# A fused attention + MLP block on one core: new order of the head, of the hidden-layer units and of the second half, and layer normalisation moved from VectorE to GpSimd

## The chip, the cores and the metric

The kernel runs on one core of a Trainium2 chip, in one launch. The metric is the device time of the launch in microseconds (us). Before the change, three runs gave a median of 188.48 us (188.34 to 201.64). One further run was taken with the hardware profiler; all trace times in this document are counted from the start of its span.

## The reference, cut to what matters

One input x of 2048 tokens by 512 channels, in bfloat16, is normalised, then goes through a linear attention with 32 heads of 16 channels and through a two-layer MLP with 1792 hidden units. Both results are added to x.

```python
xn = layernorm(x)                                # no scale, no bias
q, k, v = split(xn @ wqkv)                       # 32 heads x 16
pq, pk  = q @ w_phi[h], k @ w_phi[h]             # 16 x 16 per head
phi     = concat(softmax(+p), softmax(-p))       # for pq and for pk
kv, z   = phi_k.T @ v, sum over tokens of phi_k  # per head
attn    = (phi_q @ kv) / (phi_q . z + 1e-6)
out     = x + attn @ wo + mish(xn @ w1 + b1) @ w2
```

## The kernel before, in words

The 2048 tokens are 16 tiles of 128 (one tile in the 128 partitions), in four groups of four. The program is an order written out by hand: each engine executes its instructions strictly in the order in which the code issues them, and only semaphores between engines, and the reuse of buffers, make an engine wait. So the place of a call in the code is its place in every queue.

**The parts.** `ln_stats` (L110) takes mean and variance of some tiles on VectorE (two `bn` instructions a tile) and the reciprocal root on GpSimd (an add, L119, and a power, L122). `ln_apply` (L125, L127) writes the normalised tile `xn`, one VectorE instruction a tile. `xn` is turned into `xnT` either by TensorE (`ln_turn_pe`, four transposes and a copy; group 0) or by a DMA transpose of two tiles on SP's queue (`ln_turn_dma`, L145; groups 1 to 3). `load_turned` (L87) loads a 512 x 512 part of `wqkv` transposed by DMA (`wT`), and `fold` (L93) multiplies it with the block-diagonal `w_phi` (`Wbd`), so that one projection gives the softmax logits: `wkp` for keys, `wqp` for queries.

**Slots.** The softmaxes run in eight slots `s` of four tiles: slots 0 to 3 are the keys of groups 0 to 3, slots 4 to 7 the queries. `logits(s, i)` is one tile's projection (four matmuls of 512 columns) and a copy out of PSUM; `extremes(s)` (L194) finds maxima and minima of 16 and subtracts them (ten VectorE instructions); `exponentials(s)` (L223) is two ScalarE instructions of 128 x 2048, and for query slots also issues DMA transposes of the results (`qT`, L235) on SP; `normalise(s, k)` (L240) divides by the sums on VectorE; `accumulate(g)` (L274) adds a group's keys and values into PSUM (`pkv`). `value(t)` projects v. `hidden(n)` (L168) takes the next n of 56 *units* of the first MLP layer: four matmuls of 512 columns and one ScalarE Mish each. ScalarE reloads its table at each change between Exp and Mish.

**The second half.** `mask_kv` takes the sums out of PSUM. For each pair of tiles `h`: `attend(h, i)` (L312) multiplies `qT` with the sums (eight short matmuls into the one buffer `pnd`) and ScalarE copies the result out in four instructions (L332 to L339); `combine(h)` (L341) divides numerator by denominator in seven VectorE instructions and issues a DMA transpose of the result (`ob`, L373); `second_layer(t)` (L375) is 14 matmuls of 512 columns into a PSUM bank `po`; `project_out(h)` (L384) adds the output projection into the two banks and `residual` (L394) adds x on VectorE and issues the output's DMA.

**Buffers that matter.** One pool of five PSUM banks (tag `mm`) is shared by `fold`, transposes, `project`, `hidden` and `second_layer`: TensorE waits when the bank five allocations back hasn't been copied out. `pkv` and `pnd` share one buffer.

**Order around the change.** In the head, SP's queue issues x tiles 0-1, the transposed `wT`, x tiles 4-7, `wv`, `w1`, x tiles 8-15; ScalarE's queue issues `w_phi`, x tiles 2-3 and `b1`. TensorE runs 12 matmuls on an identity (L437), then `fold`, the turning of tiles 0 and 1, `logits(0, 0)`, tiles 2 and 3, `logits(0, 1..3)`, `value(0..3)`, `hidden(4)`. The main loop is L481, with `hidden((16, 14, 8, 10, 4)[s])`; each slot's VectorE work holds the layer normalisation of the group two ahead (of group 1 in `extremes(0)`, L472). The second half starts at L509.

Of the kernel before, what the change touches and what calls it, by code (L numbers as in the profile page):

```python
# [17 lines left out]
def kernel(  # L18
# [68 lines left out]
    def load_turned(base_col):  # L87

        wT = lnp.tile([P, 4, 512], BF16, name="wT", tag="xn")
        nc.sync.dma_start_transpose(out=wT[:], in_=A_wqkv[:, base_col : base_col + D])  # L90
        return wT

    def fold(wT, dst, dve):  # L93

        for kt in range(KT):
            pf = ps.tile([P, 512], FP32, name="pfold", tag="mm")
            for j in range(4):
                nc.tensor.matmul(
                    pf[:, j * P : (j + 1) * P],
                    lhsT=wT[:, j, kt * P : (kt + 1) * P],  # L100
                    rhs=Wbd[:, j, :],
                    start=True,
                    stop=True,
                )
# [236 lines left out]
    def combine(h):  # L341

        nm, ds = nd_of.pop(h)
        ds = ds[:].rearrange("p i l x j h -> p i l x (j h)")
        u = opool.tile([P, 2, 2, 32], FP32, name="u")
        w = opool.tile([P, 2, 32], FP32, name="w")
        f = opool.tile([P, 2, 2, 32, 2], BF16, name="f")
        ob = lnp.tile([P, 4, 512], BF16, name="ob", tag="xn")
        o_t = ob[:, 0:2, :]
        oT_of[h] = ob[:, 2:4, :].rearrange("p i (j c) -> p (i j) c", c=P)  # L350
        nc.vector.tensor_tensor(  # L351
            out=u[:], in0=ds[:, :, :, 0, :], in1=ds[:, :, ::-1, 1, :], op=ALU.mult
        )
        nc.vector.tensor_tensor(out=w[:], in0=u[:, :, 0, :], in1=u[:, :, 1, :], op=ALU.add)
        nc.vector.reciprocal(w[:], w[:])  # L355
        nc.vector.tensor_tensor(
            out=u[:], in0=ds[:, :, ::-1, 1, :],
            in1=w[:, :, None, :].to_broadcast([P, 2, 2, 32]), op=ALU.mult,
        )
        nc.vector.tensor_copy(  # L360
            f[:].rearrange("p i l c o -> p (i l c) o"),
            u[:].rearrange("p i l (c o) -> p (i l c) o", o=1).to_broadcast([P, 128, 2]),
        )
        v = nm.rearrange("p i l (c e o) -> p (i l c) e o", e=8, o=2)
        nc.vector.tensor_tensor(  # L365
            out=v, in0=v,
            in1=f[:].rearrange("p i l c o -> p (i l c) o")[:, :, None, :].to_broadcast([P, 128, 8, 2]),
            op=ALU.mult,
        )
        nc.vector.tensor_tensor(  # L370
            out=o_t, in0=nm[:, :, 0, :], in1=nm[:, :, 1, :], op=ALU.add
        )
        nc.sync.dma_start_transpose(out=oT_of[h], in_=o_t.rearrange("p i c -> p (i c)"))  # L373

    def second_layer(t):  # L375
        po = ps.tile([P, 512], FP32, name="po", tag="mm")
        po_of[t] = po
        for f in range(FT):
# [4 lines left out]

    def project_out(h):  # L384
        for i in range(2):
            po = po_of.pop(2 * h + i)
            for j in range(4):
                nc.tensor.matmul(  # L388
                    po[:], lhsT=oT_of[h][:, i * 4 + j, :], rhs=wo_sb[:, j, :],
                    start=False, stop=(j == 3),  # L390
                )
            residual(2 * h + i, po)

    def residual(t, po):  # L394
        y = x_sb[:, t, :]
        nc.vector.tensor_tensor(out=y, in0=po[:], in1=y, op=ALU.add)  # L396
        nc.sync.dma_start(o_v[:, t, :], y)


    nc.sync.dma_start(x_sb[:, 0:2, :], x_v[:, 0:2, :])  # L400
    with nc.allow_non_contiguous_dma(reason="tiny w_phi load"):
        nc.scalar.dma_start(wsrc[:], wphi_v)
# [33 lines left out]
    for _ in range(12):  # L436
        nc.tensor.matmul(  # L437
            warm[:], lhsT=ident[:], rhs=ident[:, None, :].to_broadcast([P, 4, P]),
            start=True, stop=True,
        )  # L440
# [138 lines left out]
```

## Time and profile before

| | |
|---|---|
| median of three runs | 188.48 us |
| the profiled execution's own time | 188.35 us |
| its span (first to last instruction) | 186.6 us |
| TensorE busy | 176.2 us, 94% of the span |
| VectorE busy | 148.4 us, 80% |
| ScalarE busy | 127.0 us, 68% |
| GpSimd busy | 8.2 us, 4% |
| data moved by DMA | 18.02 MB |
| table loads of ScalarE | 13 of 1.283 us |

Busy TensorE time counts from the start of a matmul to its modelled end, and matmuls overlap, so a busy engine is not yet one at its peak. A dense stream of matmuls of 512 columns starts one every 0.216 us in this trace (32 in 6.91 us). What can be gained is therefore in the gaps, and these are read from the waits of TensorE, from the chain of work that ended last, and from the timeline around each gap.

### The profile page before, as it was taken

To read this page: it belongs to the slowest core of one execution; us is meant where nothing else is said; L and a number is where in the kernel's file an instruction comes from. 1 tells how busy PE (TensorE), PEld (TensorE's weight loads), DVE (VectorE), ACT (ScalarE), POOL (GpSimd) and SP (SyncE) were. 2 spreads that over 40 slices of the span, in tenths; PEclk is the share of its full clock that TensorE was granted. 3 is DMA by queue.
4 is the path that set the end of the run, shared out by engine and by line. 5 is a ranking of instruction groups with operands and counts; after the bars stand their busy time and mean duration, and the time that the engine had idled before them with its cause. 6 is when DMAs were issued, how large, how long until landed. Compare 5 with 4: busy or idle time off the path is not lost.

```text
span 186.6 us, 2710 instructions
## 1 busy us (share of the span) xinstructions
PE 176.2 (94%) x1021; PEld 88.5 (47%) x1021; DVE 148.4 (80%) x255; ACT 127.0 (68%) x196; POOL 8.2 (4%) x22
## 2 busy tenths in 40 slices
PE   6699879999999999999999999799999999999982
PEld 2444334464444654644464555355554545455430
DVE  4989999978999899989997927299947696738742
ACT  2458999889887899969969859573842567244200
POOL 3403020000200000000000000000000000000000
PEclk9999999999999999999999999999999999999998
DMA  6996999000190000000002900973079303980732
GB/s 146 304 404 222 209 358 164 0 4 2 34 191 0 4 0 0 0 0 4 0 0 53 176 0 0 179 160 60 0 170 192 87 5 66 196 189 1 116 84 84
DMA packets 44217, 18.02 MB, mean 97 GB/s; under 512 B 36780, under 2 KB 43692, under 8 KB 44204
## 3 DMA queue, kind: packets, MB, share of 16 engines
q1 hardware_dynamic: 43376, 17.57, 40.1%
q10 hardware_dynamic: 828, 0.28, 0.6%
q8 instruction: 8, 0.13, 0.3%
q14 instruction: 5, 0.04, 0.1%
HBM read 6.84 MB, written 2.10 MB: 48 GB/s over the span
## 4 chain that ended last, share of the span: by engine, by line
PE 76%; DVE 9%; ACT 6%; DMA 5%; issue 1%; ACTq 0%; SPq 0%
PE ph L174 24%; PE pproj L154 20%; PE po L379 18%; PE po L388 6%; PE pkv L279 4%; PE pnd L323 4%; DMA ob<-ob 3%; ACT e L226 2%; DMA x_sb<-in_A_x_dram 2%; DVE stats L116 1%; DVE wv L365 1%; ACT acts L181 1%; DVE ob L370 1%; DVE w L355 1%; ACT wv L332 1%
## 5 line engine op out<-in xcount | busy, mean ns | idle before, releaser
L379 PE MATMUL po<-w_sb,acts 128*128 128x512 bf16 x224 | 50.8, 379 | 0.0
L174 PE MATMUL ph<-xnT,w_sb 128*128 128x512 bf16 x224 | 49.5, 379 | 1.2 <-ACT p_sb L192 1.2
L181 ACT ACTIVATE acts<-ph,b1f 128x512 bf16<-128x512 f32 x56 | 35.5, 694 | 3.8 <-PE ph L174 3.5
L174 PEld LDWEIGHTS <-w_sb 128*128 128x128 bf16 x224 | 21.9, 98 | 27.5 <-issue 1.4
L226 ACT ACTIVATE e<-e 128x2048 bf16<-128x2048 bf16 x16 | 29.7, 1902 | 7.0 <-DVE e L216 6.9
L379 PEld LDWEIGHTS <-acts 128*128 128x128 bf16 x224 | 21.4, 98 | 23.1
L154 PEld LDWEIGHTS <-xnT 128*128 128x128 bf16 x192 | 18.4, 98 | 22.9 <-DMA xnT<-xn 1.3
L192 ACT CAST p_sb<-pproj 128x512 bf16<-128x512 f32 x29 | 15.7, 586 | 9.7 <-PE pproj L154 9.7
L244 DVE TENSOR_REDUCE s<-e 128x128 f32<-128x2048 bf16 x8 | 18.2, 2279 | 1.6 <-ACT e L226 1.6
L396 DVE TENSOR_TENSOR x_sb<-po,x_sb 128x512 bf16<-128x512 f32 x16 | 10.6, 685 | 7.6 <-PE po L388 7.6
L388 PE MATMUL po<-wqk,ob 128*128 128x512 bf16 x64 | 15.1, 379 | 0.7 <-DMA ob<-ob 0.7
L154 PE MATMUL pproj<-wkp,xnT 128*128 128x512 bf16 x64 | 14.7, 379 | 0.8 <-DMA xnT<-xn 0.8
L154 PE MATMUL pproj<-wv,xnT 128*128 128x512 bf16 x64 | 15.1, 379 | 0.0
L332 ACT CAST wkp<-pnd 128x768 bf16<-128x768 f32 x8 | 6.4, 798 | 12.6 <-PE pnd L323 8.7
L154 PE MATMUL pproj<-wqk,xnT 128*128 128x512 bf16 x64 | 14.6, 379 | 0.2 <-DVE x_sb L396 0.2
L205 DVE TENSOR_TENSOR m<-p_sb 128x1024 bf16<-128x1024 bf16 x16 | 11.0, 686 | 3.9 <-ACT p_sb L192 3.9
L351 DVE TENSOR_TENSOR u<-ds 128x128 f32<-128x128 f32 x8 | 2.3, 289 | 12.8 <-ACT ds L339 12.8
L205 DVE TENSOR_TENSOR m<-m 128x512 bf16<-128x512 bf16 (+1 forms) x32 | 11.5, 358 | 1.1
L323 PE MATMUL pnd<-kvm,qT 128*128 128x144 bf16 x128 | 10.6, 226 | 1.1 <-ACT ds L339 1.1
L323 PEld LDWEIGHTS <-qT 128*128 128x128 bf16 x128 | 9.1, 98 | 5.0 <-issue 1.3
L116 DVE BATCH_NORM_STATS2 stats<-x_sb 128x6 f32<-128x512 bf16 x16 | 10.0, 680 | 1.2 <-DMA x_sb<-in_A_x_dram 1.2
L332 ACT CAST wv<-pnd 128x768 bf16<-128x768 f32 x8 | 6.3, 792 | 6.1 <-PE pnd L323 3.8
(64 smaller groups left out, 173.0 us busy)
## 6 DMA issues: line engine op xcount, KB each, us to landing
w_sb<-in_B_w_dram SPq DMA_DIRECT2D x2, 1792.0 KB, 8.7
out_dram<-x_sb SPq DMA_DIRECT2D x16, 128.0 KB, 1.9
x_sb<-in_A_x_dram SPq DMA_DIRECT2D x1, 1024.0 KB, 11.4
x_sb<-in_A_x_dram SPq DMA_DIRECT2D x1, 512.0 KB, 4.1
wv<-in_A_wqkv_dram SPq DMA_DIRECT2D x1, 512.0 KB, 5.0
wqk<-in_A_wo_dram SPq DMA_DIRECT2D x1, 512.0 KB
x_sb<-in_A_x_dram SPq DMA_DIRECT2D x1, 256.0 KB, 3.1
x_sb<-in_A_x_dram ACTq DMA_DIRECT2D x1, 256.0 KB, 3.5
```

Source lines behind the costliest of these rows:

```text
L116: nc.vector.bn_stats(stats[:, i, :], x_sb[:, t0 + i, :])
L154: nc.tensor.matmul(pp[:], lhsT=xnT[:, t, kt, :], rhs=w[:, kt, :], start=(kt == 0), stop=(kt == KT - 1),)
L174: nc.tensor.matmul(ph[:], lhsT=w1_sb[:, kt, f * P : (f + 1) * P], rhs=xnT[:, g * TPG : (g + 1) * TPG, kt, :], start=(kt == 0), stop=(kt == ...
L181: nc.scalar.activation(acts[:, f, g * 512 : (g + 1) * 512], ph[:], ACT.Mish, bias=b1f[:, f : f + 1])
L192: copy(p_of[s][:, i, :], pp[:])
L205: nc.vector.tensor_tensor(out=m[:], in0=src[:, :, 0:half], in1=src[:, :, half : 2 * half], op=op)
L226: nc.scalar.activation(v, v, ACT.Exp)
L244: nc.vector.reduce_sum(t[:], v.rearrange("p t l (c e) -> p (t l c) e", e=16), axis=AX.X)
L323: nc.tensor.matmul(blocks(pnd, pl, j, 144), lhsT=qT_of[h][:, i, pl * 4 + j, :], rhs=kvm[:, pl, j, :], start=True, stop=True,)
L332: nc.scalar.copy(to[:, :, 0:3, :], a)
L379: nc.tensor.matmul(po[:], lhsT=acts[:, f, t * P : (t + 1) * P], rhs=w2_sb[:, f, :], start=(f == 0), stop=False,)
L388: nc.tensor.matmul(po[:], lhsT=oT_of[h][:, i * 4 + j, :], rhs=wo_sb[:, j, :], start=False, stop=(j == 3),)
```

## The change

- **Head.** `wT` is loaded in two halves, one on SP's and one on ScalarE's DMA queue. In the built program SP's half carries a wait for the completion of ScalarE's half, and all that SP issues later stands behind it: x tiles 2-3, `wv`, x tiles 4-7, `b1`, `w1`, x tiles 8-15 (`b1` and x tiles 2-3 were on ScalarE's queue). The identity matmuls become 8. Three small copies go from VectorE to GpSimd. The four tiles of group 0 are normalised in three steps (tile 0, tile 1, tiles 2-3), with a ScalarE square root and a VectorE reciprocal instead of GpSimd's power. Tile 0 is turned between the second and third step of `fold`; `logits(0, 0)`, `logits(0, 1)` and `value(0)` come before tiles 2 and 3 are turned. `fold`'s fourth copy stays on VectorE, ahead of tile 1's normalisation.
- **Units.** `hidden` takes 5, then 19, 14, 8, 8, then 2 (before: 4, then 16, 14, 8, 10, then 4). Two of the four copies of `logits(1)` go to VectorE.
- **Normalisation.** `ln_apply` of groups 1 to 3 runs on GpSimd.
- **Second half.** `attend(0, 0)` and `attend(0, 1)` stand before `extremes(5)`, with `second_layer(1)` cut in two around the latter. `combine(3)` stands behind `project_out(2)` and no longer before it. `combine(7)` is cut into two tiles, the first before `project_out(5)`. The last tile's output projection, residual and output are cut into two halves of 256 columns, and the first half's output goes out on ScalarE's queue.

```diff
-    def load_turned(base_col):
+    def load_turned(base_col, queues=(nc.sync,)):
         wT = lnp.tile([P, 4, 512], BF16, name="wT", tag="xn")
-        nc.sync.dma_start_transpose(out=wT[:], in_=A_wqkv[:, base_col : base_col + D])
+        n = D // len(queues)
+        for i, queue in enumerate(queues):
+            queue.dma_start_transpose(
+                out=wT[:, :, i * n : (i + 1) * n],
+                in_=A_wqkv[i * n : (i + 1) * n, base_col : base_col + D],
+            )
...
-    def fold(wT, dst, dve):
+    def fold(wT, dst, dve, behind={}):
...
+            if kt in behind:
+                behind[kt]()
...
-    def ln_apply(t0, n, mv, rstd, xn, at):
+    def ln_apply(t0, n, mv, rstd, xn, at, engine=nc.vector):
         for i in range(n):
-            nc.vector.tensor_scalar(
+            engine.tensor_scalar(
...
-    def combine(h):
+    def combine(h, parts=(slice(0, 2),)):
...
+        for q in parts:
...
+            nc.sync.dma_start_transpose(
+                out=oT_of[h][:, 4 * q.start : 4 * q.stop, :],
+                in_=o_t[:, q].rearrange("p i c -> p (i c)"),
+            )
...
     def project_out(h):
         for i in range(2):
             po = po_of.pop(2 * h + i)
...
+            cuts = (slice(0, 256), slice(256, 512)) if (h, i) == (7, 1) else (slice(0, 512),)
+            for n, c in enumerate(cuts):
...
+                residual(2 * h + i, po, c, nc.sync if n or len(cuts) == 1 else nc.scalar)
...
+    nc.gpsimd.memset(eps[:], 1e-5)
     nc.sync.dma_start(x_sb[:, 0:2, :], x_v[:, 0:2, :])
     with nc.allow_non_contiguous_dma(reason="tiny w_phi load"):
         nc.scalar.dma_start(wsrc[:], wphi_v)
-    wT = load_turned(D)
-    nc.scalar.dma_start(x_sb[:, 2:4, :], x_v[:, 2:4, :])
-    nc.scalar.dma_start(b1b[:], b1_v[:, :])
+    wT = load_turned(D, (nc.sync, nc.scalar))
+    nc.scalar.activation(root[:], eps[:], ACT.Sqrt)
+    nc.sync.dma_start(x_sb[:, 2:4, :], x_v[:, 2:4, :])
+    nc.sync.dma_start(wv[:], wqkv_v[:, :, 2 * D : 3 * D])
     nc.sync.dma_start(x_sb[:, 4:8, :], x_v[:, 4:8, :])
-    nc.sync.dma_start(wv[:], wqkv_v[:, :, 2 * D : 3 * D])
+    nc.sync.dma_start(b1b[:], b1_v[:, :])
     nc.sync.dma_start(w1_sb[:], w1_v[:, :, :])
     nc.sync.dma_start(x_sb[:, 8:16, :], x_v[:, 8:16, :])
...
-    for _ in range(12):
+    for _ in range(8):
         nc.tensor.matmul(
             warm[:], lhsT=ident[:], rhs=ident[:, None, :].to_broadcast([P, 4, P]),
...
-    st0 = ln_stats(0, 2)
+    def stats_head(t, n):
...
+        for i in range(n):
+            nc.vector.bn_stats(stats[:, i, :], x_sb[:, t + i, :])
+        for i in range(n):
+            nc.vector.bn_aggr(mv[:, i, :], stats[:, i, :])
+        nc.scalar.activation(rstd[:], mv[:, :, 1], ACT.Sqrt, bias=eps[:])
+        return mv, rstd
+
+    def apply_head(t, n, mv, rstd):
+        nc.vector.reciprocal(rstd[:], rstd[:])
+        ln_apply(t, n, mv, rstd, xn, t)
+
+    st = stats_head(0, 1)
     nc.vector.tensor_tensor(
         out=Wbd[:].rearrange("p j (h e) -> p j h e", h=8),
...
-    st1 = ln_stats(2, 2)
-    xn = lnp.tile([P, TPG, D], BF16, name="xn", tag="xn")
-    ln_apply(0, 2, *st0, xn, 0)
-    fold(wT, wkp, (3,))
-    ln_turn_pe(0, xn, 0, dve)
-    ln_turn_pe(1, xn, 1, act)
+    apply_head(0, 1, *st)
+    st = stats_head(1, 1)
+    fold(wT, wkp, (3,), {1: lambda: ln_turn_pe(0, xn, 0, act)})
+    apply_head(1, 1, *st)
+    ln_turn_pe(1, xn, 1, dve)
     pb = ps.tile([P, 512], BF16, name="pb", tag="mm")
     nc.tensor.transpose(pb[:, 0:FT], b1b[:], ident[0:FT, 0:FT])
-    ln_apply(2, 2, *st1, xn, 2)
-    logits(0, 0, act)
+    st = stats_head(2, 2)
+    for i in range(2):
+        logits(0, i, act)
+    nc.vector.tensor_copy(b1f[:], pb[:, 0:FT])
+    apply_head(2, 2, *st)
+    value(0, act)
+    ln_turn_pe(2, xn, 2, dve)
+    ln_turn_pe(3, xn, 3, act)
     for i in range(2, 4):
-        ln_turn_pe(i, xn, i, dve)
-    nc.vector.tensor_copy(b1f[:], pb[:, 0:FT])
-    for i in range(1, TPG):
         logits(0, i, act)
 
     def normal(t0, st, xn):
-        ln_apply(t0, TPG, *st, xn, 0)
+        ln_apply(t0, TPG, *st, xn, 0, nc.gpsimd)
...
-    for i in range(TPG):
+    for i in range(1, TPG):
         value(i, act)
-    hidden(4)
+    hidden(5)
...
         for i in range(TPG):
-            logits(s + 1, i, act)
+            logits(s + 1, i, dve if s == 0 and i < 2 else act)
...
-        hidden((16, 14, 8, 10, 4)[s])
+        hidden((19, 14, 8, 8)[s])
...
     second_layer(0)
-    hidden(4)
+    hidden(2)
+    attend(0, 0)
+    second_layer(1, 0, 8)
+    attend(0, 1)
     extremes(5)
-    attend(0, 0)
-    second_layer(1)
-    attend(0, 1)
+    second_layer(1, 8)
     combine(0)
     exponentials(5)
...
+    first, last = (slice(0, 1),), (slice(1, 2),)
     for h in range(2 * NG):
         t = 2 * h + 4
         if h == 5:
             attend(7, 0)
-        if 0 < h < 7:
+        if h in (1, 3, 4, 5):
             combine(h + 1)
+        if h == 5:
+            combine(7, first)
+        if h == 6:
+            combine(7, last)
         project_out(h)
-        if h == 0:
-            combine(1)
+        if h in (0, 2):
+            combine(h + 1)
```

More of the change, by code (lines that the diff above doesn't have):

```diff
@@ L77 @@
     ident = consts.tile([P, P], BF16, name="ident")
+    eps = consts.tile([P, 1], FP32, name="eps")
+    root = consts.tile([P, 1], FP32, name="root")
     mhalf = consts.tile([P, TPG], FP32, name="mhalf")
@@ L308, in mask_kv @@
         )
-    nd_of, oT_of, po_of = {}, {}, {}
+    nd_of, oT_of, po_of, tmp_of = {}, {}, {}, {}
     def attend(h, i):
@@ L339, in attend @@
         nc.scalar.copy(ds[:, i, :, :, 3, :], b.rearrange("p l (x h) -> p l x h", x=2))
-    def combine(h):
-        nm, ds = nd_of.pop(h)
+    def combine(h, parts=(slice(0, 2),)):
+        nm, ds = nd_of.pop(h) if parts[-1].stop == 2 else nd_of[h]
         ds = ds[:].rearrange("p i l x j h -> p i l x (j h)")
[L345 to L378, printed above, removed]
+        if h not in oT_of:
+            ob = lnp.tile([P, 4, 512], BF16, name="ob", tag="xn")
+            u = opool.tile([P, 2, 2, 32], FP32, name="u")
+            w = opool.tile([P, 2, 32], FP32, name="w")
+            f = opool.tile([P, 2, 2, 32, 2], BF16, name="f")
+            tmp_of[h] = ob[:, 0:2, :], u, w, f
+            oT_of[h] = ob[:, 2:4, :].rearrange("p i (j c) -> p (i j) c", c=P)
@@ new lines, in combine @@
+        o_t, u, w, f = tmp_of[h]
+        for q in parts:
+            n = q.stop - q.start
+            nc.vector.tensor_tensor(
+                out=u[:, q], in0=ds[:, q, :, 0, :], in1=ds[:, q, ::-1, 1, :], op=ALU.mult
+            )
+            nc.vector.tensor_tensor(
+                out=w[:, q], in0=u[:, q, 0, :], in1=u[:, q, 1, :], op=ALU.add
+            )
+            nc.vector.reciprocal(w[:, q], w[:, q])
+            nc.vector.tensor_tensor(
+                out=u[:, q], in0=ds[:, q, ::-1, 1, :],
+                in1=w[:, q, None, :].to_broadcast([P, n, 2, 32]), op=ALU.mult,
+            )
+            nc.vector.tensor_copy(
+                f[:, q].rearrange("p i l c o -> p (i l c) o"),
+                u[:, q].rearrange("p i l (c o) -> p (i l c) o", o=1).to_broadcast(
+                    [P, n * 64, 2]
+                ),
+            )
+            v = nm[:, q].rearrange("p i l (c e o) -> p (i l c) e o", e=8, o=2)
+            nc.vector.tensor_tensor(
+                out=v, in0=v,
+                in1=f[:, q].rearrange("p i l c o -> p (i l c) o")[:, :, None, :].to_broadcast(
+                    [P, n * 64, 8, 2]
+                ),
+                op=ALU.mult,
+            )
+            nc.vector.tensor_tensor(
+                out=o_t[:, q], in0=nm[:, q, 0, :], in1=nm[:, q, 1, :], op=ALU.add
+            )
+            nc.sync.dma_start_transpose(
+                out=oT_of[h][:, 4 * q.start : 4 * q.stop, :],
+                in_=o_t[:, q].rearrange("p i c -> p (i c)"),
+            )
@@ L379, in second_layer @@
+    def second_layer(t, f0=0, f1=FT):
+        if f0 == 0:
+            po_of[t] = ps.tile([P, 512], FP32, name="po", tag="mm")
+        po = po_of[t]
+        for f in range(f0, f1):
             nc.tensor.matmul(
                 po[:], lhsT=acts[:, f, t * P : (t + 1) * P], rhs=w2_sb[:, f, :],
-                start=(f == 0), stop=False,
+                start=(f == 0), stop=(t == NT - 1 and f == FT - 1),
             )
@@ L386, in project_out, with residual @@
             po = po_of.pop(2 * h + i)
[L387 to L397, printed above, removed]
+            cuts = (slice(0, 256), slice(256, 512)) if (h, i) == (7, 1) else (slice(0, 512),)
+            for n, c in enumerate(cuts):
+                for j in range(4):
+                    nc.tensor.matmul(
+                        po[:, c], lhsT=oT_of[h][:, i * 4 + j, :], rhs=wo_sb[:, j, c],
+                        start=False, stop=(j == 3 or len(cuts) == 2), skip_group_check=len(cuts) == 2,
+                    )
+                residual(2 * h + i, po, c, nc.sync if n or len(cuts) == 1 else nc.scalar)
+    def residual(t, po, c, queue):
+        y = x_sb[:, t, c]
+        nc.vector.tensor_tensor(out=y, in0=po[:, c], in1=y, op=ALU.add)
+        queue.dma_start(o_v[:, t, c], y)
+    nc.gpsimd.memset(eps[:], 1e-5)
     nc.sync.dma_start(x_sb[:, 0:2, :], x_v[:, 0:2, :])
@@ L424 @@
     nc.vector.memset(pkv[:, :, 0:432], 0.0)
-    nc.vector.tensor_copy(KVmask[:, 0:P], block[:].rearrange("p h d -> p (h d)"))
-    nc.vector.tensor_copy(KVmask[:, P : P + 8], block[:, :, 0])
-    nc.vector.tensor_copy(
+    nc.gpsimd.tensor_copy(KVmask[:, 0:P], block[:].rearrange("p h d -> p (h d)"))
+    nc.gpsimd.tensor_copy(KVmask[:, P : P + 8], block[:, :, 0])
+    nc.gpsimd.tensor_copy(
         kvm[:].rearrange("p l j c -> p (l j) c")[:, :, 136:144],
@@ L440 @@
         )
-    st0 = ln_stats(0, 2)
+    xn = lnp.tile([P, TPG, D], BF16, name="xn", tag="xn")
+    def stats_head(t, n):
+        stats = lnp.tile([P, n, nc.vector.BN_STATS_DIM], FP32, name="hstats", bufs=3)
+        mv = lnp.tile([P, n, nc.vector.BN_AGGR_DIM], FP32, name="hmv", bufs=3)
+        rstd = lnp.tile([P, n], FP32, name="hrstd", bufs=3)
+        for i in range(n):
[8 more added lines that the diff above has]
+    st = stats_head(0, 1)
     nc.vector.tensor_tensor(
```

## The prediction, made before the changed kernel was run

> **What bounds the kernel now.** I read the page's first lines, then TensorE's lines in the view of the waits, then the timeline around each gap.
>
> ```profile
> PE 176.2 (94%) x1021; PEld 88.5 (47%) x1021; DVE 148.4 (80%) x255; ACT 127.0 (68%) x196; POOL 8.2 (4%) x22
> PEclk9999999999999999999999999999999999999998
> ```
> ```profile
> PE ph L174 <- ACT p_sb L192: 1.2, 1, 1.2
> PE pfold L98 <- DMA wT<-in_A_wqkv_dram: 1.1, 1, 1.1
> PE pnd L323 <- ACT ds L339: 1.1, 1, 1.1
> PE pproj L154 <- DMA xnT<-xn: 0.8, 1, 0.8
> PE po L388 <- DMA ob<-ob: 0.7, 2, 0.6
> PE pproj L154 <- DVE x_sb L396: 0.2, 1, 0.2
> ```
> TensorE is the bound: from 26.4 to 110 it has no gap. What is left is the head up to 26.41, 1.1 near 118, 0.2 near 143, 0.6 at 181 and the tail. The head decides, so its rows follow.
>
> ```profile
> 0.78 0.48 ACTq L402 DMA_DIRECT2D wsrc<-in_A_w_phi_dram  x1
> 1.30 3.34 SPq L90 DMA_TRANSPOSE wT<-in_A_wqkv_dram  x1
> 4.38 0.77 PEld L437 LDWEIGHTS <-ident 128*128 128x128 bf16 x4 [0.27 <-issue]
> 6.71 1.07 PE L98 MATMUL pfold<-Wbd,wT 128*128 128x128 bf16 x16 [1.06 <-DMA wT<-in_A_wqkv_dram]
> 13.71 0.69 DVE L205 TENSOR_TENSOR m<-p_sb 128x1024 bf16<-128x1024 bf16 x1
> 13.86 0.64 POOL L119 TENSOR_SCALAR rstd<-mv 128x4 f32<-128x4 f32 x1 [5.48 <-DVE mv L118]
> 16.35 3.62 PE L174 MATMUL ph<-xnT,w_sb 128*128 128x512 bf16 x16
> 20.77 3.63 PE L154 MATMUL pproj<-wkp,xnT 128*128 128x512 bf16 x16 [0.81 <-DMA xnT<-xn]
> 23.79 0.23 POOL L119 TENSOR_SCALAR rstd<-mv 128x4 f32<-128x4 f32 x1 [8.04 <-DVE mv L118]
> 26.41 7.94 PE L174 MATMUL ph<-xnT,w_sb 128*128 128x512 bf16 x36 [1.15 <-ACT p_sb L192]
> ```
> To see: `wT`, issued at 1.30, lets fold start at 6.71; the units start at 16.35; by 26.41 TensorE has done 68 matmuls of 512 columns (logits, values and units; 16 + 16 + 16 + 16 + 4) and is dense from there. The two GpSimd rows are one instruction, 0.64 with a two-input VectorE instruction beside it, 0.23 without.
>
> **The head, step by step.**
>
> *Fold.* ScalarE's half of `wT` can be issued at 1.29, behind `w_phi` (0.78 + 0.48). A half is 256 KB. Transposes of 256 KB (`xnT`) took 3.2/3.3/4.1 us (min/median/max) to land, the whole `wT` 4.4 and 5.4. I take 3.4 a half. SP's half waits for the first: 1.29 + 3.4 + 3.35 = 8.05, against 6.71 (bounds: 7.7 with 3.2 twice, 9.5 with 4.1 twice). So fold starts 1.35 later. The Trainium skill, DMA: Bandwidth & Descriptors, "Rules for kernel authors", speaks against the split: transposes from two queues have to be run one after the other, and a second queue adds no bandwidth. By it alone the split would cost one more completion. No row here shows two such transposes in flight.
>
> *SP's queue.* With 1.3 of issue for its half, x tiles 2-3 are issued at 6.0 (before 1.29) and land at 9.3 (rows: 3.1 and 3.5). `wv` and x tiles 4-7 need 1.5 each behind that (x tiles 4-7 landed at 4.70 + 4.1 = 8.8, `wv` at 5.32 + 5.0 = 10.3), so `b1`, last of the four, is there near 12.2. Its transpose stands in TensorE's queue ahead of `logits(0, 0)`, which ran at 8.98 before. `w1` follows near 17 and is hidden.
>
> *VectorE's chain.* Fold and tile 0's turning end at 9.25. Then in VectorE's order: the copy out of fold 0.69, a 128x1 reciprocal 0.16 (from 0.951 for 128 and 0.553 for 64 columns), `xn` of tile 1 0.41, on TensorE four transposes 0.39, copy 0.41: 11.4. Statistics of tiles 2-3 1.6, root on ScalarE 0.3 (nearest: its small copies, 0.215 to 0.257), reciprocal 0.2, two `xn` 0.8: 14.4. TensorE from 12.2: two logits and one value, 0.865 each, 14.8; turning 0.8, 15.5; five more projections, and the units start at 19.8 instead of 16.35: +3.4. What goes here, GpSimd's add and power (0.31 + 0.73), is paid back as root and reciprocal.
>
> *Clock.* Eight identity matmuls, 0.43 apart, end at 4.8; TensorE then idles 3.2 until 8.05 (before: 1.06). At the end of the trace the last matmul ends at 183.2 and the granted clock is 0.83 in 185.0 to 185.5 and 0.50 after: it halves after about 2.1 idle. At the start the identity matmuls stay 0.43 apart until 4.38, then run in 0.2: 3.0 of work to get it back. So I expect fold at half speed (+0.9) and then half of most of the 2.6 us of projections lost: +1.8 by the chain above (bounds 0 and 2.4). Units start at 21.55, five of them end at 25.9. The skill's TensorE: Matmul & The Clock Gate, "Part 1: The HAM clock gate", gives a free-running window of about 3.4 us. By it an idle of 3.2 could pass unpunished, and the sum would be 1.8 less; the row says 2.1 can be enough.
>
> *`xnT` of group 1.* VectorE's statistics of tiles 4-7 come after the copy of tile 2 (17.2), 2.8; GpSimd's add and power 0.64 + 1.1: 21.7. Then four `xn` on GpSimd. No row shows one. From below: 0.23 + 508 x 0.83 ns = 0.65 (memset: 128x128 0.206, 128x1 0.100); from above: 0.23 + 508 x 1.9 ns = 1.2 (affine select 128x128 0.342). All four fall into `extremes(0)`, ten two-input VectorE instructions; the row pair 0.64/0.23 prices that at 0.41 each. I take 0.65 + 0.41 = 1.06, as the memset row is the plainest stream (VectorE's own row was 0.405). If the two engines exclude each other in turn, each `xn` waits for a whole instruction and the next VectorE one for it: 2.4 more in all. Pairs are done at 23.8 and 25.9, their transposes land 3.3 later: 27.1, 29.2. TensorE waits 1.2, does two logits, waits 0.4, and has its 68 matmuls (32 + 20 + 16) at 30.9 instead of 26.41: **+4.5**. The waits of 0.8 and 1.15 of before are counted in this. The copies given to VectorE do free the banks; ScalarE (exponentials 27.8 to 31.5, table, first Mish 34.6) is then in time for the sixth unit behind (35.2). Lower end: fold at 7.7, full clock, 0.65 without contention: 27.6, +1.2. Upper end: 9.5, half clock, mutual exclusion: 34.1, +7.7.
>
> The skill's GPSIMD Engine Reference, "8. Key points", says that GpSimd shares its SBUF interfaces with VectorE instructions that have two SBUF inputs. Its "4.1 Engine selection" calls one-input work roughly line rate; by that alone an `xn` is near 0.6, and the sum some 0.8 lower.
>
> **After the head.** *Slots.* VectorE loses 12 `xn` of 1.38 per four, 4.1, and gains two copies, 1.4. TensorE has no gap there, so this buys nothing; GpSimd's other two groups have a slot's length and are hidden. VectorE's lag behind TensorE matters once: two units less (1.73) stand before `attend(0, 0)`, whose `qT` landed at 103.5 for a use at 106.3.
>
> *Near 118.* The wait of 1.06 goes: it was `attend(1, 1)` waiting for copies that stood behind `exponentials(5)`. Late next: VectorE's `combine(0)` and the one `pnd` buffer, since ScalarE must load Mish, do two units and copy before `attend(0, 1)`. Bounds 0 and 1.3 (1.06 + the 0.2 for `ob`); I take -0.7.
>
> *Near 143.* `combine(3)` behind the residuals frees the bank: -0.2. The slots' next `extremes(7)` waits for `p_sb` until 146.29, which covers it.
>
> *Tail.* `combine(7)` in halves: its last half takes 2.5 (0.22 + 0.19 + 0.35 + 0.22 + 0.22 + 0.69 + 0.42 and gaps, from the same operations at other widths) instead of 3.8, behind the first half and two residuals: done near 178.7, landed 181.1 to 181.75, needed 181.4. The wait of 0.6 mostly goes. The last residual is 256 wide, 0.42 instead of 0.69. I take -0.9 (bounds -0.3 and -1.1).
>
> **Sum.** The profiled execution took 188.35 (span 186.6 and 1.75 around it), 0.13 under the median. 188.35 + 4.5 - 0.7 - 0.2 - 0.9 = 191.05; I say **191.0**.
>
> **Rivals.**
> 1. *The head costs little, and the kernel is faster.* Mechanism: the halves land fast. Both in by 7.0 leaves 2.2 idle, no half clock, and +0.5; with gains of 1.3 + 0.2 + 1.1, 186.2. It decides where the 68th matmul ends before 28.2. For it: `wT` alone took 4.4 later on. Against: even 3.2 twice is 7.7.
> 2. *VectorE and GpSimd exclude each other.* +2.4 in the head, less what ScalarE hides: 193.0. For it: the 0.64. Against: the power row, 1.17 beside such instructions and 1.04 without.
> 3. *SP's half starts late or slowly* (4.1 twice): 191.05 + 1.4 = 192.5. For it: 3.34 of issue for the first `wT`, 1.92 for the second.
> 4. *The change doesn't do what it says:* two queues, but no two transfers at once. That is the forecast's first step.
>
> **How the numbers follow.** Forecast 0.50 (its own range 189.2 to 192.4), rival 1 0.19, rival 2 0.20, rival 3 0.11. 2% of 188.48 is 3.8, about what a measurement can tell from no change: 184.7 to 192.25. Slower by more: most of rivals 2 and 3 (0.20) and the forecast's upper edge (0.08), 0.28. Faster by more: 0.06, out of rival 1. The rest, 0.66, lies within. The range goes from rival 1's side, the lower head with the gains I took (188.35 + 1.2 - 1.8 = 187.75, with full gains 186.95), to the upper head (188.35 + 7.7 - 1.8 = 194.25): 187.3 to 194.0.
>
> **What would show it.** Right: fold starts after 7.7, on `wT`; `logits(0, 0)` after 11; a granted clock of 0.5 before 12; the first `logits(1)` after 26 on `xnT`; no wait of `pnd` near 120. Wrong: fold before 7.4, GpSimd `xn` rows under 0.6 beside full-speed VectorE rows, a gap of TensorE inside the slots, or units starting before 18.

## The result, and the profile after

The changed kernel took 202.24 us (median of four runs, 201.41 to 202.89) against 188.55 for the kernel before on the same chip: a ratio of 1.073, 95% interval 1.067 to 1.079. (One run of the kernel before, 201.64 us, lies 7% above its others and is left out of the ratio.) The forecast was 191.0, with a range up to 194.0; the kernel is 8.2 us beyond it. The profiled execution took 202.89 with a span of 201.2, 14.6 longer than before.

The page of the kernel after: engines with busy time and share, then TensorE and its granted clock in 40 slices of 5.03 us.

```profile
PE 182.5 (91%) x1006; PEld 90.8 (45%) x1021; DVE 148.9 (74%) x252; ACT 128.8 (64%) x199; POOL 33.7 (17%) x34
...
PE   7359963899999999999999998999999999999992
...
PEclk9856997579999999999999999999999999999998
```
TensorE has two holes, in the second and third slice and in the sixth and seventh, and the granted clock falls to near half in or behind each. From the tenth slice on TensorE looks as before. The waits of TensorE in the kernel after (us in total, times, longest):

```profile
PE pproj L163 <- DMA xnT<-xn: 5.9, 2, 5.2
PE pfold L105 <- DMA wT<-in_A_wqkv_dram: 3.2, 1, 3.2
...
PE ptr L148 <- DVE xn L136: 1.3, 1, 1.3
PE pb L499 <- DMA b1b<-in_B_b_dram: 0.9, 1, 0.9
PE po L413 <- DVE x_sb L421: 0.7, 1, 0.7
PE pnd L332 <- DMA qT<-e: 0.3, 1, 0.3
PE pnd L332 <- ACT ds L348: 0.3, 1, 0.3
```
The wait for `xnT` was 0.8 before and is 5.9 now; the waits for `wT` rose from 1.1 to 3.2. The wait near 118 (1.1) and the one for `ob` at 181 (0.6) are gone. In their places stand 0.3 for `qT`, 0.3 for the copies and 0.3 for `ob` ahead of the first `project_out`, and 0.7 at the end. The timeline of TensorE and GpSimd in the kernel after (start, length, instruction; the idle time before it and what ended it in brackets):

```profile
1.44 3.59 PE L464 MATMUL warm<-ident 128*128 128x512 bf16 x8 [1.44 <-POOL ident masks.py:199]
8.28 0.81 PE L105 MATMUL pfold<-Wbd,wT 128*128 128x128 bf16 x8 [3.25 <-DMA wT<-in_A_wqkv_dram]
13.28 3.59 PE L163 MATMUL pproj<-wkp,xnT 128*128 128x512 bf16 x8
23.82 4.48 PE L183 MATMUL ph<-xnT,w_sb 128*128 128x512 bf16 x20
...
24.20 10.30 POOL L136 TENSOR_SCALAR xn<-x_sb,mv,rstd 128x512 bf16<-128x512 bf16 x4
...
33.52 3.59 PE L163 MATMUL pproj<-wkp,xnT 128*128 128x512 bf16 x8 [5.22 <-DMA xnT<-xn]
37.81 1.46 PE L163 MATMUL pproj<-wkp,xnT 128*128 128x512 bf16 x3 [0.70 <-DMA xnT<-xn]
41.20 3.07 PE L183 MATMUL ph<-xnT,w_sb 128*128 128x512 bf16 x10
```
Four normalised tiles take GpSimd 10.30 us. VectorE took 1.38 for them in the kernel before:

```profile
16.69 1.38 DVE L127 TENSOR_SCALAR xn<-x_sb,mv,rstd 128x512 bf16<-128x512 bf16 x4
```
TensorE waits 5.22 for the first two of them, and then its eight matmuls take 3.59, 0.43 apart, as the identity matmuls did: half speed. The eight at 13.28 run at half speed as well. The same stretch against the kernel before and the forecast (us from the start of the span):

| | before | forecast | after |
|---|---|---|---|
| fold starts | 6.71 | 8.05 | 8.28 |
| `logits(0, 0)` | 8.98 | 12.2 | 13.28 |
| units start | 16.35 | 21.55 | 23.82 |
| first `xn` of group 1 | 16.69 | 21.7 | 24.20 |
| last `xn` of group 1 done | 18.07 | 25.9 | 34.50 |
| the 68 matmuls are done, next unit starts | 26.41 | 30.9 | 41.20 |
| first `project_out` | 118.94 | 122.7 | 134.12 |
| end of the span | 186.6 | 189.3 | 201.2 |

At 41.2 the changed kernel is 14.8 us behind, at the end 14.6. So the whole loss has arisen by 41.2, and the rest of the kernel gives back 0.2 where I had forecast 1.8.

### The profile page after: what moved, and what is told of

It is laid out like the page before. It is cut to its first block, busy times and chain, and to the rows that moved or that the text cites. A ratio compares the mean times of both kernels' runs of the same rounds, so it can differ in the third digit from the quotient of the medians.

```text
span 201.2 us, 2715 instructions
## 1 busy us (share of the span) xinstructions
PE 182.5 (91%) x1006; PEld 90.8 (45%) x1021; DVE 148.9 (74%) x252; ACT 128.8 (64%) x199; POOL 33.7 (17%) x34
## 4 chain that ended last, share of the span: by engine, by line
PE 56%; DVE 22%; DMA 8%; POOL 6%; ACT 2%; issue 2%; SPq 1%; ACTq 0%; POOLq 0%; DVEq 0%
PE po L402 18%; PE ph L183 15%; PE pproj L163 12%; PE po L413 7%; POOL xn L136 5%; DVE s L253 4%; DVE m L214 4%; DVE e L225 4%; PE pnd L332 3%; DMA b1b<-in_B_b_dram 3%; DVE e L266 2%; ACT e L235 2%; DVE r L261 2%; PE pkv L288 2%; DMA wT<-in_A_wqkv_dram 2%
## 5 line engine op out<-in xcount | busy, mean ns | idle before, releaser
L190 ACT ACTIVATE acts<-ph,b1f 128x512 bf16<-128x512 f32 x56 | 36.3, 690 | 4.9 <-PE ph L183 4.6
L235 ACT ACTIVATE e<-e 128x2048 bf16<-128x2048 bf16 x16 | 29.7, 1902 | 7.8 <-DVE e L225 7.8
L163 PEld LDWEIGHTS <-xnT 128*128 128x128 bf16 x192 | 19.5, 104 | 32.1 <-DMA xnT<-xn 7.3
L136 POOL TENSOR_SCALAR xn<-x_sb,mv,rstd 128x512 bf16<-128x512 bf16 x12 | 26.9, 2248 | 0.3
L201 ACT CAST p_sb<-pproj 128x512 bf16<-128x512 f32 x27 | 14.8, 585 | 17.4 <-PE pproj L163 11.6
L163 PE MATMUL pproj<-wkp,xnT 128*128 128x512 bf16 x62 | 19.6, 472 | 6.5 <-DMA xnT<-xn 5.9
L421 DVE TENSOR_TENSOR x_sb<-po,x_sb 128x512 bf16<-128x512 f32 (+1 forms) x17 | 10.7, 655 | 12.0 <-PE po L413 12.0
L413 PE MATMUL po<-wqk,ob 128*128 128x512 bf16 (+1 forms) x67 | 15.1, 366 | 1.0 <-DVE x_sb L421 0.7
L163 PE MATMUL pproj<-wv,xnT 128*128 128x512 bf16 x61 | 15.8, 396 | 0.2
L266 DVE TENSOR_TENSOR e<-e,r 128x2048 bf16<-128x2048 bf16 x8 | 10.7, 1337 | 0.3
L413 PEld LDWEIGHTS <-ob 128*128 128x128 bf16 x68 | 6.5, 98 | 8.2 <-issue 0.9
```

What stands on the lines that cost most here:

```text
L136: engine.tensor_scalar(out=xn[:, at + i, :], in0=x_sb[:, t0 + i, :], scalar1=mv[:, i, 0:1], scalar2=rstd[:, i : i + 1], op0=ALU.subtract, ...
L163: nc.tensor.matmul(pp[:], lhsT=xnT[:, t, kt, :], rhs=w[:, kt, :], start=(kt == 0), stop=(kt == KT - 1),)
L190: nc.scalar.activation(acts[:, f, g * 512 : (g + 1) * 512], ph[:], ACT.Mish, bias=b1f[:, f : f + 1])
L201: copy(p_of[s][:, i, :], pp[:])
L235: nc.scalar.activation(v, v, ACT.Exp)
L266: nc.vector.tensor_tensor(out=vv, in0=vv, in1=r2[:, :, None, :].to_broadcast([P, 128, 8, 2]), op=ALU.mult)
```

## The experiments

Theory A after seeing the result: GpSimd's instruction is slow by itself, 2 us and more, and the late head and the half clock add the rest. Rivals: only the contention with VectorE makes it slow; the clock alone; or the second half loses too.

### 1. The changed kernel, normalisation back on VectorE

```diff
-        ln_apply(t0, TPG, *st, xn, 0, nc.gpsimd)
+        ln_apply(t0, TPG, *st, xn, 0)
```


> The changed kernel, its layer normalisation of groups 1 to 3 back on VectorE. Theory A (an `xn` costs GpSimd 2.1 to 3.4 us, so `xnT` of group 1 comes about 9 us late, and TensorE's wait for it halves the clock a second time): `xnT` lands near 29 instead of 33.5 and 37.8, logits(1) end near 31.6 instead of 41.2, no second fall of the clock, time 192 to 193.5. Theory B (the late fold and its half clock are the main loss, GpSimd only fills a wait that is there anyway): 199 or more.

Measured: 193.87 us, 1.029 of before (1.0265 to 1.0316). One call's engine is worth 8.4 of the 13.7 us. The 68 matmuls are done at 32.14 (theory A: 31.6), 5.7 late by the head alone, and the time is 0.4 above theory A's range; theory B's 199 is far off. TensorE at the start of this kernel:

```profile
8.50 1.03 PE L105 MATMUL pfold<-Wbd,wT 128*128 128x128 bf16 x8 [3.46 <-DMA wT<-in_A_wqkv_dram]
...
13.83 3.59 PE L163 MATMUL pproj<-wkp,xnT 128*128 128x512 bf16 x8
```

### 2. The kernel before, with only the normalisation on GpSimd

```diff
-            nc.vector.tensor_scalar(
+            engine.tensor_scalar(          # nc.gpsimd for groups 1 to 3
```


> The kernel before, with only the normalisation of groups 1 to 3 on GpSimd. Theory A: `xn` runs from 15.8 to 26, `xnT` lands near 24 and 29 instead of 20.8 and 22, TensorE waits some 4 and 2 us and its clock falls to half there; 194 to 197. Theory B: the loss is in the new head and not here, 188 to 190.

Measured: 194.13, 1.031 (1.0291 to 1.0322). The timeline of this kernel:

```profile
15.97 10.31 POOL L127 TENSOR_SCALAR xn<-x_sb,mv,rstd 128x512 bf16<-128x512 bf16 x4
...
25.30 3.60 PE L154 MATMUL pproj<-wkp,xnT 128*128 128x512 bf16 x8 [5.22 <-DMA xnT<-xn]
29.55 2.19 PE L154 MATMUL pproj<-wkp,xnT 128*128 128x512 bf16 x8 [0.66 <-ACT p_sb L192]
```
The same 10.31 and the same wait of 5.22, with an early head. The price does not depend on the new head. Here it is 5.8 us; after the new head 8.4.

### 3. The changed kernel, 24 identity matmuls

```diff
-    for _ in range(8):
+    for _ in range(24):
```


> The changed kernel with 24 identity matmuls instead of 8, so that TensorE has no idle stretch before fold at 8.28. Theory C (the idle of 3.25 us halves the clock from 8.6 to 18.8, and this delays the whole head): granted clock 1.0 from 8 to 20, units start near 21.3 instead of 23.8, time 199 to 200. Rival: VectorE's chain and the loads set the head, the half clock is hidden behind them, 201.5 to 202.5.

Measured: 201.92, 1.075 (1.0707 to 1.0788): no gain clear of the noise. Theory C's 199 to 200 is out, and the rival's range holds.

```profile
9.24 0.61 PE L105 MATMUL pfold<-Wbd,wT 128*128 128x128 bf16 x8
...
13.68 3.51 PE L163 MATMUL pproj<-wkp,xnT 128*128 128x512 bf16 x8
```
The 24 matmuls themselves run until 9.4 and hold fold back to 9.24 (8.28 in the kernel after), so this run has a cost of its own and is no clean price of the clock. Fold then runs at full speed (its second eight matmuls take 0.61 instead of 1.06), but TensorE still waits 1.30 for tile 1 and 1.34 for `b1`, and with 0.70 of work in 10 to 12 and 0.66 in 12 to 14 us the granted clock falls to 0.50 at 14. The logits run 0.44 apart again (3.51 for eight). Of all this 0.7 us is left: the units start at 23.13 instead of 23.82. A clock kept for fold was lost again in the waits behind it; in experiment 9, where the wait for `b1` is gone, it is kept.

### 4. The kernel before, with only the rearranged second half

```diff
     second_layer(0)
     hidden(4)
-    extremes(5)
     attend(0, 0)
-    second_layer(1)
+    second_layer(1, 0, 8)
     attend(0, 1)
+    extremes(5)
+    second_layer(1, 8)
...
+        if h == 5:
+            combine(7, first)
+        if h == 6:
+            combine(7, last)
```
(and the order of `combine(3)` and the last tile in two halves, as in the change)

> The kernel before with only the rearranged second half (units 4, 16, 14, 8, 10, 4 as before). If the second half brings what I forecast for it (0.7 + 0.2 + 0.9): 186.5 to 187. Rival D (its waits only change places: VectorE's lag before combine(0), and the last tile's second half behind the residual of its first): 188 to 188.7.

Measured: 186.55, 0.991 (0.9895 to 0.9925). The forecast's -1.8 for the second half holds when the two units stay. Its parts come out differently: the first `project_out` starts at 117.69 (-1.25; I took -0.7), from there to the `project_out` of the last pair but one 59.53 instead of 59.89 (-0.36; I took -0.2), and from there to the end 7.58 instead of 7.77 (-0.2; I took -0.9). The waits of TensorE and the tail of this kernel:

```profile
PE po L404 <- DVE x_sb L412: 0.7, 1, 0.7
```
```profile
180.02 1.02 DVE L412 TENSOR_TENSOR x_sb<-po,x_sb 128x512 bf16<-128x512 f32 x2 [0.17 <-PE po L404]
...
181.09 0.60 PE L404 MATMUL po<-wqk,ob 128*128 128x256 bf16 x4 [0.68 <-DVE x_sb L412]
181.72 0.42 DVE L412 TENSOR_TENSOR x_sb<-po,x_sb 128x256 bf16<-128x256 f32 x1 [0.69 <-PE po L404]
```
The last tile's second half waits 0.68 until VectorE has read its first half: both lie in one bank, and the code issues the first residual between them.

### 5. The changed kernel, normalisation on VectorE, loads as before

```diff
-    wT = load_turned(D, (nc.sync, nc.scalar))
+    wT = load_turned(D)
+    nc.scalar.dma_start(x_sb[:, 2:4, :], x_v[:, 2:4, :])
+    nc.scalar.dma_start(b1b[:], b1_v[:, :])
     nc.scalar.activation(root[:], eps[:], ACT.Sqrt)
-    nc.sync.dma_start(x_sb[:, 2:4, :], x_v[:, 2:4, :])
...
-    nc.sync.dma_start(b1b[:], b1_v[:, :])
```


> The changed kernel with the normalisation back on VectorE and the loads in their old order and on their old queues (the whole of wT on SP, x tiles 2-3 and b1 on ScalarE's queue); the new order of the head's work, the units and the second half are kept. Theory A, the loads make the head late (fold at 8.50 and b1 at 13.7 in the first experiment): fold starts at 6.6 to 7.0, logits(0, 0) before 10.5 at full speed, the 68th matmul ends before 28.5, and the time falls from 193.87 to 187.5 to 190. Theory B, the finer order of the head (tile by tile, root on ScalarE) is slow by itself: fold is early, but the logits still wait for the chain on VectorE, the 68th matmul ends after 30, and the time stays above 191.5.

Measured: 190.55, 1.011 (1.0098 to 1.0128), between the two theories: the loads are worth 3.3 us, but not all of the head. TensorE in this kernel:

```profile
6.74 0.62 PE L105 MATMUL pfold<-Wbd,wT 128*128 128x128 bf16 x8 [1.71 <-DVE hmv L478]
...
9.34 0.61 PE L148 MATMUL ptr<-ident,xn 128*128 128x128 bf16 x4 [1.30 <-DVE xn L136]
...
10.00 3.59 PE L163 MATMUL pproj<-wkp,xnT 128*128 128x512 bf16 x8
13.38 1.89 PE L163 MATMUL pproj<-wv,xnT 128*128 128x512 bf16 x4
```
Fold is early and at full speed (0.62 for eight), yet the projections run at half speed, with a granted clock of 0.50 from 10 to 14. Theory B's chain is there too: tile 1 waits for VectorE (1.30), where the copy out of fold stands ahead of its normalisation.

### 6. The second half alone, and the new units

```diff
-            logits(s + 1, i, act)
+            logits(s + 1, i, dve if s == 0 and i < 2 else act)
...
-        hidden((16, 14, 8, 10, 4)[s])
+        hidden((19, 14, 8, 8)[s])          # 5 before the loop, 2 behind it
```


> The kernel before with the rearranged second half (186.55 in the last experiment) and now also the new counts of units (5, 19, 14, 8, 8, 2) and two of the copies of logits(1) on VectorE; head and normalisation as before. Theory A, the units cost nothing and the two copies take away the wait of 1.15 us at 26.4: 185.4 to 186.2. Theory B, the units ahead move the same wait to another place or make VectorE late for the slots: 186.5 to 188.

Measured: 186.85, 0.992 (0.9902 to 0.9931): 0.3 above experiment 4, with overlapping intervals. Theory A's gain is out, as theory B has it; a loss is not shown by the times. The second half of this kernel shows where the gain goes:

```profile
105.95 0.67 PE L323 MATMUL pnd<-kvm,qT 128*128 128x144 bf16 x8 [0.46 <-DMA qT<-e]
...
108.79 0.66 PE L323 MATMUL pnd<-kvm,qT 128*128 128x144 bf16 x8 [0.44 <-ACT ds L339]
```
With two units less ahead of `attend(0, 0)`, its `qT` is no longer covered, and neither are the copies for `attend(0, 1)`. Neither wait is in experiment 4, nor in experiment 12, which has the two copies alone. The changed kernel has the same two, 0.33 and 0.33.

### 7. The second half alone, both halves of the last projection ahead of the residuals

```diff
+            for n, c in enumerate(cuts):
                 residual(2 * h + i, po, c, ...)
```
(the second loop stands behind the one over the matmuls)

> The kernel before with the rearranged second half, and in the last output projection the matmuls of both halves of 256 columns now stand before the two residuals. Theory A, the second half's wait of 0.68 us for the first residual is on the path to the end: 0.3 to 0.7 less than the 186.55 of the rearranged second half alone, so 185.9 to 186.25. Theory B, the end is set by the first residual and by the output's DMA, which now start later by the second half's matmuls: 186.4 to 186.8.

Measured: 186.10, 0.9875 (0.9858 to 0.9891), 0.45 below experiment 4: theory A. From the `project_out` of the last pair but one to the end it takes 7.1 instead of 7.58. Only so are the two halves worth most of what I had booked for them.

### 8. GpSimd's price by itself

```python
for i in range(4): on_pool(g_alone[:, i, :], x_sb[:, i, :])            # the form of the change
for i in range(4): on_pool(g_half[:, i, 0:256], x_sb[:, i, 0:256])
...
for i in range(8): on_pool(g_two[:, i, :], x_sb[:, i, :])    # VectorE: 20 maxima, 128x1024
for i in range(8): on_pool(g_single[:, i, :], x_sb[:, i, :]) # VectorE: 40 copies, 128x1024
```


> A kernel that leaves out the whole computation (its output is x) and only times GpSimd: the normalising instruction of 128 x 512 with two scalars from memory, with VectorE idle; the same at 256 columns; with two immediate scalars; with one operation; a plain copy; then the first form again beside two-input maxima of 128 x 1024 on VectorE, and beside plain copies there; last the maxima with GpSimd idle. Theory A, the form is slow by itself: about 2.0 us with VectorE idle, about 1.0 at 256 columns, 2.3 to 3.4 beside the maxima, and the maxima at 1.0 to 1.3 instead of about 0.69. Theory B, it is fast by itself (0.65 to 1.06, as I had priced it) and only the contention makes it 2 us and more: 0.65 to 1.1 with VectorE idle.

Between the lines shown stand four each with two immediate scalars, with one operation, and a plain copy. This kernel was executed once. Its groups (count, busy us, mean ns of one, idle before):

```profile
L74 POOL TENSOR_SCALAR g_single<-x_sb,mv 128x512 bf16<-128x512 bf16 x8 | 21.9, 2749 | 0.1
L74 POOL TENSOR_SCALAR g_two<-x_sb,mv 128x512 bf16<-128x512 bf16 x8 | 21.8, 2739 | 0.0
L112 DVE COPY v_single<-g_two 128x1024 bf16<-128x1024 bf16 x40 | 19.2, 557 | 0.0
L103 DVE TENSOR_TENSOR v_two<-g_copy,x_sb 128x1024 bf16<-128x1024 bf16 x20 | 14.9, 816 | 28.0 <-POOL g_copy L97 28.0
L74 POOL TENSOR_SCALAR g_alone<-x_sb,mv 128x512 bf16<-128x512 bf16 x4 | 8.2, 2072 | 9.5 <-DVE mv L71 9.5
L87 POOL TENSOR_SCALAR g_imm<-x_sb 128x512 bf16<-128x512 bf16 x4 | 7.6, 1922 | 0.0
L92 POOL TENSOR_SCALAR g_one<-x_sb,mv 128x512 bf16<-128x512 bf16 x4 | 6.2, 1560 | 0.0
L115 DVE TENSOR_TENSOR v_free<-g_single,x_sb 128x1024 bf16<-128x1024 bf16 x8 | 5.0, 682 | 1.9 <-POOL g_single L74 1.9
L74 POOL TENSOR_SCALAR g_half<-x_sb,mv 128x256 bf16<-128x256 bf16 x4 | 4.8, 1219 | 0.0
L97 POOL COPY g_copy<-x_sb 128x512 bf16<-128x512 bf16 x4 | 2.3, 612 | 0.0
```
Theory A. Alone, with VectorE idle, the instruction takes 2.07: (2072 - 1219) / 256 = 3.3 ns a column and 0.37 us fixed. The plain copy of the same tile takes 0.61, one operation 1.56, two with immediate scalars 1.92. So it is the operations that are slow on GpSimd, not the moving of the tile; whether the arithmetic itself or a conversion of numbers around it takes the time, no run separates. Contention adds to it and does not explain it. One GpSimd instruction beside the maxima took up to 3.43, beside the copies 2.84 in the middle of the stretch, and the last three of `g_two`, with VectorE done, 2.07 again.

### 9. Experiment 5 with 12 identity matmuls

```diff
-    for _ in range(8):
+    for _ in range(12):
```


> The changed kernel with the normalisation on VectorE and the old loads (190.55 in the last experiments), now with 12 identity matmuls instead of 8. There fold started at 6.74 already, but the first twelve projections ran 0.43 us apart, and the granted clock was 0.50 from 10 to 14. Theory A, the half clock is most of what is left: with 12 the projections run at 0.216 from 10.0 on, the wait for the tiles 2-3 gives back a part, and the time falls by 1.3 to 2.3, to 188.2 to 189.3. Theory B, the chain on VectorE (1.71 and 1.30 us of waiting) halves the clock again or decides by itself: less than 0.7 is gained, 189.8 or more.

Measured: 188.27, 0.9987 (0.9975 to 0.9998): 2.3 less than with 8, theory A. TensorE in this kernel:

```profile
6.93 0.62 PE L105 MATMUL pfold<-Wbd,wT 128*128 128x128 bf16 x8 [0.83 <-DMA wT<-in_A_wqkv_dram]
...
9.53 0.40 PE L148 MATMUL ptr<-ident,xn 128*128 128x128 bf16 x4 [1.30 <-DVE xn L136]
...
9.97 1.90 PE L163 MATMUL pproj<-wkp,xnT 128*128 128x512 bf16 x8
...
18.08 4.48 PE L183 MATMUL ph<-xnT,w_sb 128*128 128x512 bf16 x20
```
The same wait of 1.30, the same start of the logits at 10, and eight of them in 1.90 instead of 3.59. It is not that eight identity matmuls are too few to bring the clock up: fold behind them ran at full speed in the profiled execution of experiment 5 too (0.62 for eight in both). There the granted clock fell at 8.30, after 3.4 us in which TensorE had worked 1.44. Twelve end at 6.11 instead of 5.02, TensorE works 2.08 in the like stretch (5.31 to 8.72), and the clock stays.

### 10. Experiment 1 with `b1` back on ScalarE's queue

```diff
     wT = load_turned(D, (nc.sync, nc.scalar))
+    nc.scalar.dma_start(b1b[:], b1_v[:, :])
...
-    nc.sync.dma_start(b1b[:], b1_v[:, :])
```


> The changed kernel with the normalisation on VectorE (193.87), b1 alone moved back to ScalarE's queue, behind its half of wT; the halves, and the other loads on SP, stay. There b1 landed for 13.7 and kept the logits for 0.98 us. Theory A, the late b1 costs its wait: logits(0, 0) at about 12.9 and 192.6 to 193.2. Theory B, the halves of wT are what is late, and b1 hides behind the same chain on VectorE: 193.5 to 194.2. If theory B holds, the 3.3 us that the old loads gave back are all wT's.

Measured: 192.45, 1.021 (1.0164 to 1.0254), a little below theory A's range; its runs lie between 191.83 and 193.58, so the gain of 1.4 us on experiment 1 is rough. TensorE in this kernel:

```profile
8.33 0.62 PE L105 MATMUL pfold<-Wbd,wT 128*128 128x128 bf16 x8 [3.29 <-DMA wT<-in_A_wqkv_dram]
...
11.97 3.59 PE L163 MATMUL pproj<-wkp,xnT 128*128 128x512 bf16 x8
```
It no longer waits for `b1`, and the logits start at 11.97 instead of 13.83. Of these 1.86 us, 0.98 is the wait for `b1`; most of the rest is the clock of the two profiled executions, since fold's first eight matmuls took 1.03 in experiment 1 and 0.62 here. So `b1`'s place behind three large loads is worth 1.0 to 1.4 of the 3.3 us of the loads. The rest is left for the halves of `wT` and for x tiles 2-3 behind them, which no run separates.

### 11. Experiment 7, groups 2 and 3 on GpSimd

```diff
-        ln_apply(t0, TPG, *st, xn, 0)
+        ln_apply(t0, TPG, *st, xn, 0, nc.vector if t0 == TPG else nc.gpsimd)
```


> The best kernel so far (before, with the rearranged second half and both halves of the last projection ahead of the residuals: 186.10), and groups 2 and 3, not group 1, normalised on GpSimd. Theory A, as forecast: TensorE has no gap in the slots, and GpSimd has a slot's length: 185.8 to 186.4, with VectorE less busy by some 2 us. Theory B, the GpSimd instructions slow VectorE beside them and make it late for a slot or for the second half: 186.6 to 188.

Measured: 185.98, 0.986 (0.9838 to 0.9881), not to be told from experiment 7. In the slots the 8.4 us that GpSimd takes for a group are hidden, and VectorE's time was not needed there: theory A. VectorE's busy time is 148.0 us, against 149.4 in experiment 7: eight instructions of 0.405 are gone, 3.2, so the others took some 1.8 longer beside GpSimd.

### 12. Experiment 7, two copies of `logits(1)` on VectorE

```diff
-            logits(s + 1, i, act)
+            logits(s + 1, i, dve if s == 0 and i < 2 else act)
```


> The best kernel so far (186.10) with two of the copies of logits(1) on VectorE; the counts of units stay as before. Theory A, it was these copies that took away the wait of 1.15 us at 26.4 when units and copies were changed together, and the new waits there (0.60 and 0.2 at 27 to 30, 0.5 and 0.4 in the second half) came from the counts of units: 185.0 to 185.7. Theory B, the wait only moves behind the next units, since ScalarE is busy to 34 us without a break: 185.9 to 186.4.

Measured: 185.87, 0.985 (0.9831 to 0.9872), 0.23 below experiment 7 with overlapping intervals: inconclusive, at the edge of theory B. The wait of 1.15 at 26 is gone, and 0.3 + 0.3 stand in its place. It has the lowest median of all, but is not to be told from experiments 7 and 11.

## Why the prediction was wrong, by its own steps

The differences of the runs, in order, from 188.4: the second half -1.85 (experiment 4); units and copies +0.3 (6); the new order of the head +1.4 (9 against 6); 8 identity matmuls instead of 12 +2.3 (5 against 9); the loads +3.3 (1 against 5); GpSimd +8.4 (after against 1). They are differences of neighbours, so that they add up to the 202.24 measured proves nothing; each is a difference of two medians whose intervals are 0.2 to 1.1 us either way, and the +0.3 is not clear of that. The parts depend on their order: GpSimd alone costs 5.8. What makes up the +1.4 of the new order, no run separates; in experiment 9 TensorE waits 1.30 for tile 1.

**The step that failed: the price of `xn` on GpSimd.** "From below: 0.23 + 508 x 0.83 ns = 0.65 (memset ...); from above: 0.23 + 508 x 1.9 ns = 1.2 (affine select ...)"; "I take 0.65 + 0.41 = 1.06". Measured: 2.07 alone and 2.58 on average in the head. The contention, 0.41 each, came out at 0.51 on average, but by luck: the four took 3.39, 2.82, 2.07 and 2.07, so two bore all of it and two none. The instruction's own rate was wrong, 2.07 against 0.65, and my upper bound of 1.2, on which the end of the range rested, was far too low. I took two rows that do no arithmetic with two scalars, a memset and an affine select, as bounds for one that does. Two rows of the same trace gave a warning: over the same four columns the add took 0.23 and the power 1.04, so GpSimd's time goes by the operation and not only by the bytes. Four instructions make 10.30 instead of 4.24, +6.1 us. The rest of the gap of 10.3 at the 68th matmul is 2.5 of a later start (24.20 against 21.7), and 1.7 behind the last `xn` (6.7 to the next unit instead of 5.0), which is the second stretch at half clock: TensorE waited 5.22, the granted clock is 0.62 in 32 to 34 and 0.50 from there to 42. That this wait would cost the clock as well was in none of my cases. The first four signs that I had named for being right came true (the fifth did not: `pnd` waits at 122 and 125), and yet the time was far off, since none of them was an upper limit for a GpSimd row: I had named a row under 0.6 as a sign of being wrong, and none over 1.2.

The Trainium skill, GPSIMD Engine Reference, "4.1 Engine selection", calls one-input work on GpSimd roughly line rate. The runs agree for the plain copy, 0.61 us, and not for the normalising instruction, 2.07; the measurement decides. (The prediction put the sum 0.8 lower by that section alone. Its own chain gives 1.2: at an estimated 0.6 each the first pair is done at 22.9 and lands at 26.2, and four logits from there end at 29.7 instead of 30.9.)

**Fold** (8.05): right, 8.28, on `wT`, after an idle of 3.25. SP's half was issued at 4.88, 3.6 behind ScalarE's at 1.29: two queues, and one transfer at a time. So rival 3, a late or slow half, came to 0.2.

**SP's queue** (`logits(0, 0)` at 12.2): right in kind, 1.1 too early; `b1` kept TensorE until 13.16. Experiment 10 puts its price at 1.0 to 1.4.

**Clock** (+1.8, bounds 0 and 2.4): right in kind, and for the reason given: between 5.16 and 8.57 TensorE worked 0.29 us in the kernel after, the granted clock fell there, and the logits ran at half speed. Experiments 5 and 9, with the loads as before, give 2.3 for the four identity matmuls. What I had not seen is that less idle is enough: in experiment 5 it was 1.71, with fold behind it, and the clock fell as well.

**Near 118** (-0.7): right in kind where the units stay (-1.25), and used up by the two units that I let go at no price; "whose `qT` landed at 103.5 for a use at 106.3" was too little cover. In the changed kernel the old waits, 1.06 + 0.18, became 0.33 + 0.33 + 0.26, and the half clock beyond 41.2 takes some 0.7 back (ten matmuls in 3.07): 134.12 - 118.94 is 15.2, against 14.8 at 41.2.

**Near 143** (-0.2): right in kind, -0.35; 59.54 from the first `project_out` to the last-but-one pair, 59.89 before. **Tail** (-0.9): -0.23; the wait for `ob` went, as forecast, and the wait for the residual in the same bank, which I had not looked for, took its place. **Slots** ("so this buys nothing"): right, by experiment 11.

**The rivals.** Number 2, mutual exclusion, put the loss at the right place for a wrong reason: GpSimd was slow with VectorE idle. Number 1 was out from the start, since fold began at 8.28.

## What to carry to other kernels

Before work goes to another engine, find a row of that engine doing the same operation at the same width; rows of fills and copies did not bound arithmetic here (0.65 and 1.2 against 2.07). Where there is no such row, time the instruction in a small kernel first, as experiment 8 does. A wait on TensorE in a sparse stretch is to be priced with the clock that it costs: 5.2 us of waiting cost some 2 more (1.7 up to the next unit, 0.7 behind it). And count what a moved or shortened piece of work covered, down to two units of 0.86 us.
